# Attention rows in padded pairs, one division per tile, remainder loads doubled

## The chip, the cores and the metric

The kernel runs on one core of a Trainium2 chip. The metric is the device time of one execution in microseconds (us). Five engines work side by side, each in the order of its own instructions: TensorE (PE; its weight loads are listed as PEld), VectorE (DVE), ScalarE (ACT), GpSimd (POOL) and SyncE (SP), which here issues nearly all plain transfers. Engines wait for each other through semaphores.

## The reference

Pooled attention feeds a mixture of experts. All numbers are fp32.

```python
k_p = k.reshape(B, H, Sp, pool, D).mean(axis=3)        # 8, 8, 72, 64: eight rows pooled to one
v_p = v.reshape(B, H, Sp, pool, D).mean(axis=3)
scores = scale * np.matmul(q, k_p.transpose(0, 1, 3, 2))
attn = np.exp(scores - np.max(scores, axis=-1, keepdims=True))
attn = attn / (np.sum(attn, axis=-1, keepdims=True) + 1e-09)
x = np.matmul(attn, v_p)          # then (8, 8, 576, 64) -> x [4608, 512]
logits = x @ w_gate + modality_bias[modality_id]       # 8 experts
e_idx = np.argmax(logits, axis=1)                      # one expert per token
gate_w = softmax(logits)[e_idx]
out[mask_e] = gate_w * (np.maximum(x[mask_e] @ w1[e], 0.0) @ w2[e])   # 512 -> 1024 -> 512
```

q, k and v are 8 batches x 8 heads x 576 rows x 64.

## The kernel before, in words

The order of the work on each engine is the order in which the program is written; no scheduler moves it.

**Attention steps.** A tile is 128 rows of q for all eight heads. There are 36 tiles in 20 steps. A batch has 576 rows: 512 of them are four tiles in two steps (two tiles each), and the remaining 64 rows of two neighbouring batches make one mixed step with one tile. The main loop runs over the steps `n`. In iteration `n` it issues loads and stores (`loads(n)`), finishes step `n-1` (transposes of its probabilities `t_pe`, products with the pooled v `a_pe`, division `x_dve`) and carries step `n` and `n+1` through scores (`s_pe`), row maximum and subtraction (`s_dve`, L515 and L518) and exponentials (`s_act`).

**k and v.** Each batch's k and v come as a bulk load of 1024 KB (512 rows of all heads, L201 and L217) and a remainder load of the last 64 rows (`load_k4`, L208, 128 KB; `load_v4`, L224, twice 128 KB). GpSimd pools eight rows to one by three additions (`fold`, L296 to L298), VectorE pools a part (L301), and TensorE transposes the pooled k (`pk`, L330; L333 for the remainder) and v (`pv`, L362; L363). The two remainder tiles have one buffer each. Which loads stand in which iteration is given by the table `step_loads`; after them `loads(n)` issues the stores queued so far. SP issues all of these in order, and each transfer takes one of eight semaphores in turn, so a transfer is not issued before the one eight places ahead has landed.

**av and the division.** `a_pe` writes one tile's eight heads into two PSUM tiles of one bank each, `av0` and `av1` (four heads each; per head 64 values, 8 gate logits and the sum of the probabilities). `x_dve` divides each half by four VectorE instructions: L595 scales the sums, L597 takes their reciprocals `r`, L599 multiplies the values into the row buffer `xb`, L601 the logits into `lg`.

**Routing.** From `lg` small VectorE operations choose each token's expert, gate weight and place (L648 to L773). They wait in a list `drip`; `gap(n)` puts the next n of them into VectorE's order at that point. In `x_dve` a `gap(1)` stands before the reciprocal and another before the multiplication of each half.

**xs.** The rows of x go to a DRAM tile `xs` of 4608 rows, XW = 513 words each: 512 values and the gate weight, which four later transfers per group write in pieces of 4 bytes (L681, L683). A batch's 512 rows are stored at once, as 2048-byte pieces. The MoE gathers 128 rows at a time from `xs` by an indirect transfer.

**MoE.** Tokens are sorted into slots of 256 with one expert each. Per slot and per slice `f` of 128 hidden units TensorE does twelve hidden matmuls (`first`, L163: hp, in high and low parts), ScalarE writes `hh` (the high part of the rectified hidden values, L165), VectorE `hlo` (the rest, L167), and TensorE does six matmuls of the second layer (L1102: op). The hidden matmuls of slice f+1 stand ahead of the second-layer matmuls of slice f. The two hidden buffers are

```python
hp = [ps_av.tile([P, 512], F32, tag=f"av{i}", name=f"hp{i}") for i in range(2)]
```

The last slot (`end`) does its last five slices with the second layer of only half the tokens between them, and the other half behind.

Of the kernel before, what the change touches and what calls it, by code (L numbers as in the profile page):

```python
# [22 lines left out]
P = 128  # L23
# [7 lines left out]
def kernel(  # L31
# [25 lines left out]
    XW = D + 1  # L57
# [126 lines left out]
    with ExitStack() as actx:  # L184
# [21 lines left out]
        def load_k4(b):  # L206
            k4raw[b] = ap.tile([64, POOL * HD], F32, tag="k4", bufs=1, name=f"k4_{b}")
            nc.sync.dma_start(k4raw[b], rows_of(k, b)[NCH * P:, :])  # L208
# [261 lines left out]
        qts, pqs, scs, pes, pps, pts, avs, xb, lgs = {}, {}, {}, {}, {}, {}, {}, {}, {}  # L470
# [87 lines left out]
        def a_pe(t):  # L558
# [3 lines left out]
            av = [ps_av.tile([P, 512], F32, tag=f"av{u}", name=f"av_{t}_{u}") for u in range(2)]  # L562
# [5 lines left out]
            for u in range(2):  # L568
                for gg in range(2):
                    c = 2 * u + gg  # L570
                    for hs, y in halves:
                        nc.tensor.matmul(av[u][hs, 2 * VC * gg:2 * VC * (gg + 1)], pt[:, c, hs],  # L572
                                         vw[y][:, c].rearrange("p a x -> p (a x)"), start=(gg == 0), stop=False)
                dst4 = av[u][:, 0:4 * VC].rearrange("p (g x) -> p g x", g=2)[:, :, VC:2 * VC]
# [3 lines left out]
        def x_dve(t):  # L578
# [5 lines left out]
            if (gi in (0, 5)):  # L584
                xb[b] = late_p.tile([P, 4, D], F32, tag="xb", bufs=2, name=f"xb_{b}")
            if mixed:
                xb[b, 4] = late_p.tile([P, D], F32, tag="xb4", bufs=1, name=f"xb4_{b}")
            if gi == 0:
                lgs[g] = late_p.tile([P, GT, H, E], F32, tag="lg", bufs=2, name=f"lg_{g}")
            xo = xb[b, 4] if mixed else xb[b][:, gi % 5, :]  # L590
            for u in range(2):
                avv = av[u][:, 0:4 * VC].rearrange("p (h x) -> p h x", h=4)
                r = ap.tile([P, 4], F32, tag="r", bufs=4, name=f"r_{t}_{u}")
                rb = r.rearrange("p (h o) -> p h o", o=1)
                nc.vector.tensor_scalar(r, avv[:, :, VC - 1], float(POOL), 1e-9 * POOL, op0=ALU.mult, op1=ALU.add)  # L595
                gap(1)
                nc.vector.reciprocal(r, r)  # L597
                gap(1)
                nc.vector.tensor_tensor(xo[:, u * D // 2:(u + 1) * D // 2].rearrange("p (h d) -> p h d", h=4), avv[:, :, 0:HD],  # L599
                                        rb.to_broadcast([P, 4, HD]), op=ALU.mult)  # L600
                nc.vector.tensor_tensor(lgs[g][:, gi, 4 * u:4 * u + 4, :], avv[:, :, HD:HD + E],  # L601
                                        rb.to_broadcast([P, 4, E]), op=ALU.mult)

            if mixed:
                for z in range(2):
                    r0 = (b - 1 + z) * S + 512
                    stores.append(lambda z=z, r0=r0: nc.sync.dma_start(xs[r0:r0 + 64, 0:D], xo[64 * z:64 * z + 64, :]))
            if gi in (3, 8):
                stores.append(lambda: nc.sync.dma_start(
                    xs[b * S:b * S + 512, 0:D].rearrange("(p j) x -> p j x", j=4), xb[b]))  # L610
# [226 lines left out]
        for n, fn, b in ((0, load_k4, 1), (0, load_v4, 1), (0, load_k, 2), (0, load_v, 2), (0, load_k, 3), (1, load_q, 2),  # L837
                         (1, load_k4, 2), (1, load_v, 3), (1, load_k, 4), (2, load_qmix, 1), (2, load_v4, 2), (2, load_v, 4),
                         (3, load_k4, 3), (3, load_k, 5), (4, load_q, 3), (4, load_v4, 3), (4, load_v, 5), (5, load_k4, 4),
# [391 lines left out]
```

## Time and profile before

| | us |
|---|---|
| median of 3 runs | 654.39 (651.99 to 654.73) |
| profiled execution | 655.11 |
| its span | 653.4 |

| engine | busy us | share of the span |
|---|---|---|
| TensorE matmuls | 614.3 | 94% |
| TensorE weight loads | 557.2 | 85% |
| VectorE | 430.7 | 66% |
| ScalarE | 340.8 | 52% |
| GpSimd | 191.7 | 29% |

The span has two parts: attention with routing up to about 200 us, and the MoE slots behind it. Shares over the whole span mix the two, so each stage is read by itself. In rows of the timeline, the brackets say how long the engine had been idle and what ended that. TensorE's granted clock is 1.00 at full speed.

### The profile page before, as it was taken

To read this page: it belongs to the slowest core of one execution; us is meant where nothing else is said; L and a number is where in the kernel's file an instruction comes from. 1 tells how busy PE (TensorE), PEld (TensorE's weight loads), DVE (VectorE), ACT (ScalarE), POOL (GpSimd) and SP (SyncE) were. 2 spreads that over 40 slices of the span, in tenths; PEclk is the share of its full clock that TensorE was granted. 3 is DMA by queue.
4 is the path that set the end of the run, shared out by engine and by line. 5 is a ranking of instruction groups with operands and counts; after the bars stand their busy time and mean duration, and the time that the engine had idled before them with its cause. 6 is when DMAs were issued, how large, how long until landed. Compare 5 with 4: busy or idle time off the path is not lost.

```text
span 653.4 us, 12655 instructions
## 1 busy us (share of the span) xinstructions
PE 614.3 (94%) x4313; PEld 557.2 (85%) x4313; DVE 430.7 (66%) x963; ACT 340.8 (52%) x625; POOL 191.7 (29%) x228
## 2 busy tenths in 40 slices
PE   4499999899799999999999999999999999999993
PEld 3389898888698999999999999999999999999982
DVE  4577889899977665665565666566566656656540
ACT  2447665577451454454555555555555555555530
POOL 5388774753000211311211312220221221121121
PEclk9889999899999999999999999999999999999998
DMA  9999999995402821101101253101115410110120
GB/s 256 247 352 248 320 209 265 231 263 137 108 19 64 259 81 50 66 4 63 57 15 60 91 183 113 64 34 34 66 50 175 162 55 17 49 65 17 50 71 16
DMA packets 65404, 76.55 MB, mean 117 GB/s; under 512 B 15407, under 2 KB 42031, under 8 KB 65328
## 3 DMA queue, kind: packets, MB, share of 16 engines
q1 hardware_dynamic: 59088, 55.68, 32.0%
q0 software_dynamic: 6240, 19.95, 9.2%
q8 instruction: 36, 0.59, 0.4%
q14 instruction: 40, 0.33, 0.2%
HBM read 119.64 MB, written 19.42 MB: 213 GB/s over the span
## 4 chain that ended last, share of the span: by engine, by line
PE 70%; DMA 12%; DVE 7%; SPq 4%; issue 4%; POOL 1%; ACT 1%; POOLq 0%; DVEq 0%; ACTq 0%
PE op L1102 27%; PE hp L163 27%; DMA out_dram<-ob,sidx 7%; PE av L572 4%; DMA v<-in_v_dram 3%; PE xt L154 2%; PE sc L508 2%; PE ph L163 2%; PE av L576 2%; PE pp L537 1%; PE ptab L1008 1%; DVE hl L139 1%; DMA q<-in_q_dram 1%; PE pq L483 1%; SPq L241 1%
## 5 line engine op out<-in xcount | busy, mean ns | idle before, releaser
L136 ACT CAST hl<-raw 128x1024 fp32r<-128x1024 f32 x138 | 145.1, 1051 | 142.9 <-PE op L1102 140.9
L163 PE MATMUL hp<-xh,hl 128*128 128x256 f32 x1152 | 186.0, 284 | 0.4 <-issue 0.4
L163 PEld LDWEIGHTS hp<-xh,hl 128*128 128x128 f32 x1152 | 166.1, 189 | 11.5 <-issue 0.9
L139 DVE TENSOR_TENSOR hl<-raw,hl 128x1024 fp32r<-128x1024 f32 x144 | 174.9, 1216 | 0.0
L1102 PE MATMUL op<-hl,hh 128*128 128x512 f32 x556 | 174.2, 394 | 0.0
L1088 POOL DMA_INDIRECT out_dram<-ob,sidx x38 | 52.7, 1387 | 378.6 <-DVE ob L1084 269.7
L167 DVE SCALAR_TENSOR_TENSOR hlo<-hp,hh 128x256 fp32r<-128x256 f32 x139 | 58.9, 424 | 139.7 <-ACT hh L165 128.9
L1102 PE MATMUL op<-hl,hlo 128*128 128x512 f32 x278 | 108.9, 392 | 0.0
L1102 PEld LDWEIGHTS op<-hl,hh 128*128 128x128 f32 x556 | 95.2, 189 | 12.3
L163 PE MATMUL hp<-xl,hl 128*128 128x256 f32 x576 | 92.0, 282 | 0.0
L165 ACT ACTIVATE hh<-hp 128x256 fp32r<-128x256 f32 x139 | 53.2, 383 | 49.7 <-PE hp L163 47.8
L163 PEld LDWEIGHTS hp<-xl,hl 128*128 128x128 f32 x576 | 78.9, 190 | 0.0
L1102 PEld LDWEIGHTS op<-hl,hlo 128*128 128x128 f32 x278 | 52.2, 188 | 11.8
L572 PE MATMUL av<-vw,pt 128*128 128x146 f32 (+1 forms) x320 | 52.4, 307 | 3.0 <-DVE r L595 1.6
L143 POOL DMA_INDIRECT xg<-xs,gidx x40 | 42.8, 1071 | 17.8 <-issue 9.5
L572 PEld LDWEIGHTS av<-vw,pt 128*128 128x128 f32 (+1 forms) x320 | 41.5, 188 | 5.5 <-DVE lg L601 1.9
L508 PE MATMUL sc<-kt,qt 128*128 128x144 f32 x256 | 38.7, 296 | 1.4 <-DVE sb L518 1.3
L515 DVE TENSOR_REDUCE mx<-sc 128x8 f32<-128x576 f32 (+1 forms) x40 | 27.7, 693 | 15.4 <-ACT pt L556 8.6
L508 PEld LDWEIGHTS sc<-kt,qt 128*128 128x128 f32 x256 | 34.7, 198 | 2.2 <-issue 1.5
L157 DVE TENSOR_TENSOR xl<-xt,xh 128x512 fp32r<-128x512 f32 x38 | 24.6, 686 | 17.5 <-ACT xh L156 17.5
L542 ACT COPY pt<-pp 128x512 f32<-128x512 f32 x36 | 21.1, 585 | 28.6 <-PE pp L537 28.3
L576 PE MATMUL av<-vw,pt 128*128 128x146 f32 (+1 forms) x160 | 31.1, 299 | 0.5 <-ACT pt L556 0.5
(225 smaller groups left out, 716.9 us busy)
## 6 DMA issues: line engine op xcount, KB each, us to landing
raw<-in_moe_w_dram SPq DMA_DIRECT2D x304, 256.0 KB
xs<-xb SPq DMA_DIRECT2D x8, 1024.0 KB
k<-in_k_dram SPq DMA_DIRECT2D x7, 1024.0 KB
v<-in_v_dram SPq DMA_DIRECT2D x7, 1024.0 KB
q<-in_q_dram SPq DMA_DIRECT2D x6, 1024.0 KB
q<-in_q_dram SPq DMA_DIRECT2D x4, 512.0 KB
v<-in_v_dram SPq DMA_DIRECT2D x16, 128.0 KB
k<-in_k_dram SPq DMA_DIRECT2D x4, 256.0 KB
```

The lines of the kernel that those rows point to most:

```text
L136: nc.scalar.copy(hl[f][:, 0, :], raw[f])
L139: eng.tensor_sub(hl[f][:, 1, :], raw[f], hl[f][:, 0, :].bitcast(F32))
L143: nc.gpsimd.indirect_dma_start(out=xgs[(2 * s + tt) % len(xgs)], out_offset=None, in_=xs[0:rows, :], in_offset=IndirectOffsetOnAxis(idx[:, ...
L163: nc.tensor.matmul(ph, hl[f][:, w, d * P:(d + 1) * P], x[:, d, :], start=(n == 0 and d == 0), stop=(n == 2 and d == ND - 1))
L165: nc.scalar.activation(hh, ph, AF.Relu)
L167: nc.vector.scalar_tensor_tensor(hlo, ph, 0.0, hh.bitcast(F32), op0=ALU.max, op1=ALU.subtract)
L508: nc.tensor.matmul(dst, qt[:, i, :], kt[b % NB][:, :, h * SPL:(h + 1) * SPL], start=True, stop=True)
L515: nc.vector.reduce_max(mx, scv, axis=AX.X)
L572: nc.tensor.matmul(av[u][hs, 2 * VC * gg:2 * VC * (gg + 1)], pt[:, c, hs], vw[y][:, c].rearrange("p a x -> p (a x)"), start=(gg == 0), sto ...
L576: nc.tensor.matmul(dst4[hs], pt4[:, hs], v4[y][:, 2 * u:2 * u + 2, :], start=False, stop=True)
L1088: nc.gpsimd.indirect_dma_start(out=out[:, :], out_offset=IndirectOffsetOnAxis(idx.bitcast(U32), 0), in_=ob, in_offset=None, bounds_check=N ...
L1102: nc.tensor.matmul(o[tt], l[:, ts_], hl[f][:, w, D:2 * D], start=(f == 0 and n == 0), stop=(f == NF - 1 and n == 2))
```

## The change

It has five parts.

1. Rows of `xs` become 528 words wide. The row buffer `xb` becomes a tile [128, 2, 528] per step, eleven tiles in all; GpSimd sets their last 16 words to zero at the start, and each step stores its two tiles' rows as one transfer of 4224 contiguous bytes per partition. The store now writes the gate's word too, so gate transfers wait for it.
2. The remainder tiles of k and v get two buffers each. Their loads stand one batch earlier in the table, and those of batch 1 directly behind k and v of batch 1.
3. The routing inputs (`load_routing`, five small transfers of modality ids and bias) are loaded in iteration 1 and not before the loop, and their preparation on VectorE (`routing_constants_2`) moves from iteration 1 to 3.
4. `av` becomes one PSUM tile of two banks, and a tile's eight heads are divided by four instructions in place of eight. The routing operations stand behind them (`gap(4)`), not between.
5. The MoE's two hidden buffers become halves of one tile.

```diff
-    XW = D + 1
+    XW = D + 16
...
-            k4raw[b] = ap.tile([64, POOL * HD], F32, tag="k4", bufs=1, name=f"k4_{b}")
+            k4raw[b] = ap.tile([64, POOL * HD], F32, tag="k4", bufs=2, name=f"k4_{b}")
...
-            t4 = ap.tile([P, POOL * HD], F32, tag="v4", bufs=1, name=f"v4_{b}")
+            t4 = ap.tile([P, POOL * HD], F32, tag="v4", bufs=2, name=f"v4_{b}")
...
+        NX0 = 8
+        xbs = [cp.tile([P, 2, XW], F32, tag=f"raw{i}", name=f"xb{i}") for i in range(NX0)]
+        xbs += [late_p.tile([P, 2, XW], F32, name=f"xb{NX0 + i}") for i in range(3)]
+        for t in xbs:
+            nc.gpsimd.memset(t[:, :, D:XW], 0.0)
...
-            av = [ps_av.tile([P, 512], F32, tag=f"av{u}", name=f"av_{t}_{u}") for u in range(2)]
+            av = ps_av.tile([P, 2, 512], F32, tag="av", name=f"av_{t}")
...
+            xw = xbs[n if n < NX0 else NX0 + n % (len(xbs) - NX0)]
+            xo = xw[:, z, 0:D]
+            avv = av[:, :, 0:4 * VC].rearrange("p u (h x) -> p u h x", h=4)
+            r = ap.tile([P, 2, 4], F32, tag="r", bufs=4, name=f"r_{t}")
...
+            nc.vector.tensor_scalar(r, avv[:, :, :, VC - 1], float(POOL), 1e-9 * POOL, op0=ALU.mult, op1=ALU.add)
+            nc.vector.reciprocal(r, r)
...
+            gap(4)
...
+            elif z == 1:
+                jj = steps[n][1]
                 stores.append(lambda: nc.sync.dma_start(
-                    xs[b * S:b * S + 512, 0:D].rearrange("(p j) x -> p j x", j=4), xb[b]))
+                    xs[b * S:b * S + 512, :].rearrange("(p j) x -> p j x", j=4)[:, 2 * jj:2 * jj + 2, :], xw))
...
         load_gate()
         load_k(1)
+        load_k4(1)
         load_qmix(0)
         routing_constants()
         load_v(1)
+        load_v4(1)
         load_q(1, (0,))
         load_q(1, (1,))
-        load_routing()
...
-        for n, fn, b in ((0, load_k4, 1), (0, load_v4, 1), (0, load_k, 2), (0, load_v, 2), (0, load_k, 3), (1, load_q, 2),
+        for n, fn, b in ((0, load_k, 2), (0, load_k4, 2), (0, load_v, 2), (0, load_v4, 2), (0, load_k, 3), (1, load_q, 2),
...
-            if n == 1:
+            if n == 3:
                 routing_constants_2()
...
-    hp = [ps_av.tile([P, 512], F32, tag=f"av{i}", name=f"hp{i}") for i in range(2)]
+    hp2 = ps_av.tile([P, 2, 512], F32, tag="av", name="hp")
+    hp = [hp2[:, i, :] for i in range(2)]
```

How this moves instructions is seen at three places. The first is SP's order behind the load of k for batch 1 (`k_1` and `v_1` are the remainder tiles of batch 1, `qm` the mixed step's rows of q, `mod` and `mb` the routing inputs; DMAHW0 to 7 are the eight transfer semaphores). Before:

```order
L201 DMA k_169<-in_k_dram 128x4x512 [waits DMAHW5_49]
L241 DMA qm_171<-in_q_dram 64x8x64 [waits DMAHW6_49]
L241 DMA qm_171<-in_q_dram 64x8x64 [waits DMAHW7_49]
L217 DMA v_186<-in_v_dram 128x4x512 [waits DMAHW0_49]
L234 DMA q_188<-in_q_dram 128x8x128 [waits DMAHW1_49]
L234 DMA q_188<-in_q_dram 128x8x128 [waits DMAHW2_49]
L398 DMA mod<-in_moe_modality_id_dram 128x4x8 [waits DMAHW3_49]
L400 DMA mod<-in_moe_modality_id_dram 64x4x2 [waits DMAHW4_49]
L398 DMA mod<-in_moe_modality_id_dram 128x4x8 [waits DMAHW5_49]
L400 DMA mod<-in_moe_modality_id_dram 64x4x2 [waits DMAHW6_49]
L403 DMA mb<-in_moe_modality_bias_dram 128x16 [waits DMAHW7_49]
L208 DMA k_1_262<-in_k_dram 64x512 [waits DMAHW0_49,DVE_49]
```

And now:

```order
L201 DMA k_191<-in_k_dram 128x4x512 [waits DMAHW5_49]
L208 DMA k_1_193<-in_k_dram 64x512 [waits DMAHW6_49]
L241 DMA qm_195<-in_q_dram 64x8x64 [waits DMAHW7_49]
L241 DMA qm_195<-in_q_dram 64x8x64 [waits DMAHW0_49]
L217 DMA v_210<-in_v_dram 128x4x512 [waits DMAHW1_49]
L224 DMA v_1_212<-in_v_dram 64x1x512 [waits DMAHW2_49]
L224 DMA v_1_212<-in_v_dram 64x1x512 [waits DMAHW3_49]
L234 DMA q_215<-in_q_dram 128x8x128 [waits DMAHW4_49]
L234 DMA q_215<-in_q_dram 128x8x128 [waits DMAHW5_49]
L201 DMA k_282<-in_k_dram 128x4x512 [waits DMAHW6_49]
```

The remainder of k for batch 1 moves from behind the five routing transfers to directly behind k, that of v directly behind v.

The second is VectorE's order around one division with routing operations. Before, one tile (rows L650 to L658 are routing):

```order
L595 TENSOR_SCALAR r_0_1013<-av_0_986 128x4 [waits PE_49]
L650 TENSOR_REDUCE m_0_945<-lgr_943 128x9 [waits DVE_49]
L597 RECIPROCAL r_0_1013<-r_0_1013 128x4 [waits DVE_49]
L653 TENSOR_TENSOR lgr_943<-lgr_943,m_0_945 128x72 [waits DVE_49]
L599 TENSOR_TENSOR xb_1011<-av_0_986,r_0_1013 128x256 [waits DMAHW1_49,DVE_49]
L601 TENSOR_TENSOR lg_1012<-av_0_986,r_0_1013 128x32
L595 TENSOR_SCALAR r_1_1021<-av_1_987 128x4 [waits PE_49]
L657 SCALAR_TENSOR_TENSOR lgr_943<-lgr_943,w_166 128x72 [waits Activation_49]
L597 RECIPROCAL r_1_1021<-r_1_1021 128x4 [waits DVE_49]
L658 TENSOR_REDUCE m_0_946<-lgr_943 128x9 [waits DVE_49]
L599 TENSOR_TENSOR xb_1011<-av_1_987,r_1_1021 128x256 [waits DVE_49]
L601 TENSOR_TENSOR lg_1012<-av_1_987,r_1_1021 128x32
```

And now, one tile with the routing operations that follow it:

```order
L598 TENSOR_SCALAR r_1198<-av_1168 128x8 [waits PE_49]
L599 RECIPROCAL r_1198<-r_1198 128x8 [waits DVE_49]
L600 TENSOR_TENSOR xb_174<-av_1168,r_1198 128x512 [waits DVE_49]
L602 TENSOR_TENSOR lg_982<-av_1168,r_1198 128x64
L698 CAST rki_923<-rk_922 128x9
L699 TENSOR_SCALAR rkm_924<-rki_923 128x9 [waits DVE_49]
L700 TENSOR_SCALAR rki_923<-rki_923 128x9 [waits DVE_49]
L701 CAST rkf_925<-rkm_924 128x9
L702 CAST rh<-rki_923 128x9 [waits DVE_49]
```

Eight instructions with routing between them have become four with routing behind them.

The third is TensorE's order in the MoE, at two neighbouring slices. Before:

```order
L163 MATMUL hp_2867<-xh_2857,hl_2105 128x256 x4
L163 MATMUL hp_2867<-xl_2858,hl_2105 128x256 x4
L163 MATMUL hp_2867<-xh_2857,hl_2105 128x256 x4
L1102 MATMUL op_0_2864<-hl_1983,hh_2868 128x512 [waits Activation_49]
L1102 MATMUL op_0_2864<-hl_1983,hh_2868 128x512
L1102 MATMUL op_0_2864<-hl_1983,hlo_2870 128x512 [waits DVE_49]
L1102 MATMUL op_1_2865<-hl_1983,hh_2868 128x512 x2
L1102 MATMUL op_1_2865<-hl_1983,hlo_2870 128x512
L163 MATMUL hp_2866<-xh_2857,hl_2107 128x256 x4
```

And now:

```order
L163 MATMUL hp<-xh_87,hl_1750 128x256 [waits DVE_49]
L163 MATMUL hp<-xh_87,hl_1750 128x256 x3
L163 MATMUL hp<-xl_88,hl_1750 128x256 x4
L163 MATMUL hp<-xh_87,hl_1750 128x256 x4
L1107 MATMUL op_0_2664<-hl_1646,hh_2669 128x512 [waits Activation_49]
L1107 MATMUL op_0_2664<-hl_1646,hh_2669 128x512
L1107 MATMUL op_0_2664<-hl_1646,hlo_2671 128x512
L1107 MATMUL op_1_2665<-hl_1646,hh_2669 128x512 x2
L1107 MATMUL op_1_2665<-hl_1646,hlo_2671 128x512
L163 MATMUL hp<-xh_87,hl_1864 128x256 [waits DVE_49]
```

The wait for VectorE (for `hlo` of the slice before) has moved from the second-layer matmul that uses `hlo` up to the first hidden matmul of the next slice, since both hidden buffers are one tile.

More of the change, by code (lines that the diff above doesn't have):

```diff
@@ L583, in x_dve @@
             b = steps[n][0]
[L584 to L587, printed above, removed]
             if gi == 0:
                 lgs[g] = late_p.tile([P, GT, H, E], F32, tag="lg", bufs=2, name=f"lg_{g}")
[L590 to L602, printed above, removed]
@@ L609, in x_dve @@
+            gap(4)
+            if mixed:
+                for y in range(2):
+                    r0 = (b - 1 + y) * S + 512
+                    stores.append(lambda y=y, r0=r0: nc.sync.dma_start(xs[r0:r0 + 64, :], xw[64 * y:64 * y + 64, 0, :]))
+            elif z == 1:
+                jj = steps[n][1]
                 stores.append(lambda: nc.sync.dma_start(
-                    xs[b * S:b * S + 512, 0:D].rearrange("(p j) x -> p j x", j=4), xb[b]))
+                    xs[b * S:b * S + 512, :].rearrange("(p j) x -> p j x", j=4)[:, 2 * jj:2 * jj + 2, :], xw))
```

27 lines of the change are left out of this document (14 added, 13 removed).

## The prediction

> **What bounds the kernel now.** First the busy time by stages, in stretches that follow the stages (all views are of the kernel before; columns: stretch and length, then busy us of each engine with instructions, TensorE's granted clock, DMA share, GB/s):
>
> ```profile
> 20.00:40.00 20.00, 11.84 (x73) 9.84 (x71) 9.62 (x25) 6.68 (x18) 11.08 (x14) 0.74 0.95 293
> 40.00:85.00 45.00, 43.79 (x367) 40.52 (x366) 38.74 (x141) 29.52 (x79) 34.63 (x45) 1.00 1.08 300
> 85.00:121.00 36.00, 33.45 (x281) 29.74 (x279) 32.49 (x117) 23.34 (x61) 22.63 (x30) 1.00 1.12 236
> 121.00:140.00 19.00, 17.38 (x141) 15.97 (x141) 16.30 (x50) 12.08 (x31) 12.93 (x17) 0.91 0.97 195
> 140.00:180.00 40.00, 34.90 (x287) 31.61 (x289) 37.94 (x132) 24.81 (x61) 8.42 (x11) 0.96 0.57 158
> 180.00:640.00 460.00, 459.56 (x3115) 418.96 (x3112) 284.13 (x487) 236.50 (x361) 89.27 (x72) 1.00 0.23 72
> ```
>
> From 180 to 640 TensorE is never idle (0.44 us of 460), so nothing there can be gained by this change and every new wait costs in full. In 40 to 180 TensorE idles 1.21 + 2.55 + 1.62 + 5.10 = 10.5 us: that is the ceiling for faster divisions and stores, and in the last of these stretches VectorE is the fuller engine (37.94 of 40). In 20 to 40 TensorE idles 8.16 us and runs at clock 0.74. Second, who TensorE waited for (us in total, times, longest):
>
> ```profile
> PE pk L333 <- POOL kp L298: 6.2, 1, 6.2
> ...
> PE av L572 <- DVE r L595: 1.6, 1, 1.6
> PE av L572 <- DVE lg L601: 1.4, 3, 0.9
> PE pv L363 <- POOL vp L298: 1.1, 1, 1.1
> ```
>
> One wait of 6.2 us stands out. Third, the timeline around it (start, length, engine, line, tiles; SPq rows are the issuing queue), and the data rate from 15 to 50 us in 40 slices of 0.875 us:
>
> ```profile
> 19.86 3.76 SPq L398 DMA_DIRECT2D mod<-in_moe_modality_id_dram  x1
> 26.79 0.49 SPq L208 DMA_DIRECT2D k<-in_k_dram  x1
> 19.98 0.72 POOL L296 TENSOR_TENSOR k<-k 128x256 f32<-128x256 f32 x1 [1.53 <-DMA k<-in_k_dram]
> 29.85 0.72 POOL L296 TENSOR_TENSOR k<-k 64x256 f32<-64x256 f32 x1 [8.21 <-DMA k<-in_k_dram]
> 25.07 0.27 PE L330 MATMUL pk<-ident,kp 128*64 128x128 f32 x1 [0.21 <-DVE vw L383]
> 37.22 0.32 POOL L298 TENSOR_TENSOR vp<-v 128x64 f32<-128x64 f32 x1
> 31.53 0.31 PE L333 MATMUL pk<-ident,kp 64*64 64x64 f32 x1 [6.19 <-POOL kp L298]
> 31.78 1.34 PE L572 MATMUL av<-vw,pt 128*128 128x146 f32 x4
> 34.85 1.06 PE L537 MATMUL pp<-ident,pe 128*128 128x128 f32 x4
> 38.17 0.66 PE L572 MATMUL av<-vw,pt 128*128 128x146 f32 x4
> 39.66 0.60 PE L537 MATMUL pp<-ident,pe 128*128 128x128 f32 x4
> 41.43 0.38 PE L362 MATMUL pv<-ident,vp 128*128 128x128 f32 x2
> GB/s 288 384 349 177 220 246 328 380 341 297 291 284 126 20 23 188 197 159 363 391 332 372 398 393 400 386 377 362 364 356 314 222 272 360 386 389 384 362 212 182
> ```
>
> The remainder rows of k for batch 1 (the 64-partition load of L208) are issued at 26.79, behind five routing loads that hold SP from 19.86, and behind their dip in the rate (20 and 23 GB/s). GpSimd, idle for 8.21, folds them at 29.85, and TensorE's transpose starts at 31.53.
>
> **The early remainder load: -6.2, -1.6 and -1.1.** Now this load is the row behind k's own. GpSimd was waiting at 19.98 for exactly k's load, so k has landed by then; the remainder of 128 KB at some 300 GB/s (the slices above) comes 0.5 us later, GpSimd ends its present fold at 21.6 (1.34 us for the same three operations at 19.98 to 21.64) and has folded the remainder at about 23.3. TensorE asks for it at 25.34 (25.07 + 0.27). The 6.2 us go. After the stall the same work ran slow: from the four av matmuls at 31.78 to the four pp at 34.85 is 3.07 us, from 38.17 to 39.66 it is 1.49, so 1.58 us more go with the low clock. What is late next is v of batch 1. GpSimd's six fold operations for it follow those of k's remainder, from 31.5 to 37.54 (37.22 + 0.32), and TensorE transposes the result at 41.43, which would become 33.65. They can start once v has landed: behind k come now its remainder, the mixed rows of q and v itself, 0.13 + 0.26 + 1.05 MB, at some 0.3 MB per us 4.8 us after 19.98, so 24.8; folded by 30.9, 2.8 us to spare. q of batch 1 is pushed back by 0.39 MB, 1.3 us: the rate falls at 25.5, when all that was queued had landed, so q lands at about 26.8; its transposes stand just before the av matmuls at 38.17, that is at about 30: hidden. The 1.1 us at L363 is a later remainder of v, now loaded a batch earlier, and goes too: its fold was held by its load.
>
> The routing loads go to iteration 1, between the remainder of k for batch 3 and all of k for batch 4. Their dip, some 2.6 us (three slices), then delays loads needed three batches on: 0. Bounds: 0 to +2.6 us (one dip reaching TensorE once). SP now also waits for GpSimd and VectorE at the double-buffered tiles, whose earlier users (batch 0) are done by 18: 0.
>
> **The division: -1, between -5 and +4.** By form (count, busy us, mean ns, idle before):
>
> ```profile
> L518 DVE TENSOR_TENSOR sb<-sc,mx 128x576 f32<-128x576 f32 x30 | 22.6, 754 | 0.7
> L518 DVE TENSOR_TENSOR sb<-sc,mx 128x288 f32<-128x288 f32 x8 | 3.6, 453 | 0.1
> 89.42 0.15 DVE L595 TENSOR_SCALAR r<-av 128x4 f32<-128x4 f32 x1
> 89.49 0.17 DVE L695 CAST rki<-rk 128x9 int32<-128x9 f32 x1
> 89.61 0.18 DVE L597 RECIPROCAL r<-r 128x4 f32<-128x4 f32 x1
> ...
> 90.26 0.15 DVE L595 TENSOR_SCALAR r<-av 128x4 f32<-128x4 f32 x1
> ```
>
> A half takes 0.84 us from start to start (89.42 to 90.26), with or without a routing operation in it, because those start in the gaps that the dependent operations leave (89.49, before the reciprocal at 89.61). A tile is 1.68. From 288 to 576 elements L518 grows by 0.301 us, so 256 to 512 costs 0.27 more: the new tile takes 0.84 + 0.27 and some 0.05 for the wider small ones, 1.16, a saving of 0.52. With 36 tiles that is 18.7 us of VectorE, but most lies where TensorE is the bound. In routing stretches up to four operations of about 0.1 us lose their free places, so only 0.1 of the 0.52 is left: over some 20 tiles -2. Against that, TensorE's next av matmul was released by the first half, 0.84 after the start, and now by the whole tile, 1.16 after it: 0.3 later, wherever it waited closely (the lg rows of the wait list: 3, and about as many more with hardly any slack): +1. The lower end is half of the 10.5 us idle; the upper is twelve such tiles at 0.3.
>
> **Stores, padding, memsets: 0, between -3 and +4.** Wider rows make 3% more bytes. One contiguous store per step replaces 2048-byte pieces; the gate's four-byte writes stay, but the later ones now wait for the store just before, and SP stands in that wait ahead of k's and q's loads. These are one to two batches ahead, so 0; four such waits with 1 us each reaching TensorE are the upper end. Eleven memsets on GpSimd lie before its first fold, in its wait for v: 0.
>
> **The shared hidden tile: +4.8.** In the MoE the two hidden buffers become halves of one tile, and the first hidden matmul of every slice now carries a wait for VectorE (for hlo of the slice before):
>
> ```profile
> L167 DVE SCALAR_TENSOR_TENSOR hlo<-hp,hh 128x256 fp32r<-128x256 f32 x139 | 58.9, 424 | 139.7 <-ACT hh L165 128.9
> 312.87 0.43 DVE L167 SCALAR_TENSOR_TENSOR hlo<-hp,hh 128x256 fp32r<-128x256 f32 x1 [1.23 <-ACT hh L165]
> 313.40 0.41 PEld L163 LDWEIGHTS hp<-xh,hl 128*128 128x128 f32 x2
> 313.62 0.28 PE L163 MATMUL hp<-xh,hl 128*128 128x256 f32 x1
> 629.97 0.66 PEld L163 LDWEIGHTS hp<-xh,hl 128*128 128x128 f32 x4
> 631.26 0.42 DVE L167 SCALAR_TENSOR_TENSOR hx<-hp,hx 128x256 fp32r<-128x256 f32 x1 [3.81 <-ACT hx L165]
> 632.10 0.67 PEld L163 LDWEIGHTS hp<-xh,hl 128*128 128x128 f32 x4
> 632.25 0.43 DVE L167 SCALAR_TENSOR_TENSOR hx<-hp,hx 128x256 fp32r<-128x256 f32 x1 [0.57 <-ACT hx L165]
> ```
>
> In the steady loop hlo ends at 313.30, 0.10 before the weight load and 0.32 before the matmul: just hidden, 0. In the last slot the second matmuls cover only half as much: hx ends at 631.68 where the weight load now starts at 629.97 (+1.7 and, with the load no longer ahead of the matmul, +0.1), and at 632.68 against 632.10; the next three slices have the same gap of 0.58, of which some 0.5 shows each: 1.8 + 1.5 = 3.3. Slot 1, with routing still on VectorE, adds about 1, and three slices with hlo late by 0.3 the rest, estimates by the same gap: 4.8.
>
> **Sum**, against the profiled execution of 655.11 (span 653.4; median of the runs 654.39, 0.7 lower, which I leave): 655.1 - 6.2 - 1.6 - 1.1 - 1.0 + 4.8 = 650.0.
>
> **Rivals.** *The wait breaks the steady loop.* The load leads its matmul by 0.22 us (313.40, 313.62). If a matmul with a wait can't have its weights loaded ahead, 139 slices pay up to 0.22: +30.6, so 680; half of it gives 665. Decided by hlo's signal arriving later than 0.10 after its end. For: the margin is that thin. Against: in the kernel before the second-layer matmul on hlo carries such a wait, long satisfied, and its weights load ahead. *Another load takes the place of the stall.* v of batch 1, or a load behind SP's wait for a store, is late by most of what was won; the data rate near its ceiling until 140 speaks for it, the 2.8 us to spare against it: 650.0 + 6, 656. *More is won in the routing stretches.* A routing operation stalls inside a division:
>
> ```profile
> 97.33 2.32 DVE L722 TENSOR_SCALAR rot<-iota_f,e 128x8 f32<-128x8 f32 x1
> 97.26 2.35 POOL L296 TENSOR_TENSOR v<-v 128x1024 f32<-128x1024 f32 x1
> L686 DVE TENSOR_TENSOR cum<-cum,dc 128x8 bf16<-128x8 bf16 x3 | 2.4, 783 | 0.0
> ```
>
> If moving it behind the division, off the path of the av tile, saved the stall (2.3 and some 2 in cum), the time would be 645.5. But the operation ends at 99.65 and GpSimd's at 99.61: the stall goes with the neighbour, and then it holds the next row maximum. The Trainium skill ("SBUF — State Buffer", section "SBUF: two separate sides") states that VectorE and GpSimd share one port pair as an exclusive lock, held for the whole instruction; by that rule the move gains nothing here and the sum stays at 650.0, and the two ends 0.04 us apart agree.
>
> **How the numbers follow.** 0.5% is 3.3 us, about what a measurement can tell from no change: under 651.1 is faster, over 657.7 slower. The sum as it stands 0.50, own range 646 to 654 (0.32 faster, 0.18 same); the broken loop 0.13 (slower); another load 0.16 (half same, half slower); more won 0.17 (faster); the rest 0.04, split. So faster 0.51, same 0.26, slower 0.23. The range runs from 641 (more won, with the division's lower end) to 662 (another load, with the stores' upper end), leaving out most of the broken loop.
>
> **What would show it.** The wait of the L333 transpose on GpSimd gone and the clock of 20 to 40 near 1; the first transposes of v for batch 1 without a wait; a division of 1.1 to 1.2 us per tile; waits of hidden matmuls on VectorE in the last slot of about 3 us, and none in the middle. I am wrong if 300 to 600 us holds fewer slices than before, or if TensorE waits for a load before 140.

## The result: slower by 0.9%

| | before | changed |
|---|---|---|
| median of 16 runs, us | 654.69 | 660.75 |
| lowest and highest, us | 651.99, 665.57 | 657.44, 666.22 |
| profiled execution's span, us | 653.4 | 660.9 |
| ratio to before, with its 95% interval | | 1.0094 [1.0073, 1.0116] |

The forecast was 650.0, faster. The change is slower by about 6 us. Below, times of one session are compared by their ratio to runs of the kernel before in the same session, since its level moved between sessions (medians 654.7 to 658.7).

### The profile page after: what moved, and what is told of

It reads as the page before. It is cut to its first block, busy times and chain, and to the rows that moved or that the text cites. A ratio compares the mean times of both kernels' runs of the same rounds, so it can differ in the third digit from the quotient of the medians.

```text
span 660.9 us, 12527 instructions
## 1 busy us (share of the span) xinstructions
PE 620.1 (94%) x4313; PEld 561.1 (85%) x4313; DVE 428.6 (65%) x819; ACT 340.7 (52%) x625; POOL 193.1 (29%) x239
## 4 chain that ended last, share of the span: by engine, by line
PE 68%; DMA 13%; DVE 11%; issue 4%; ACT 2%; SPq 1%; POOL 1%; POOLq 0%; DVEq 0%; ACTq 0%
PE hp L163 27%; PE op L1107 26%; DMA out_dram<-ob,sidx 7%; DMA k<-in_k_dram 5%; PE av L579 3%; PE xt L154 2%; PE sc L515 2%; PE ph L163 2%; PE av L583 2%; DVE mx L522 1%; DVE sb L525 1%; DVE arow L704 1%; PE ptab L1013 1%; PE pp L544 1%; DVE hl L139 1%
## 5 line engine op out<-in xcount | busy, mean ns | idle before, releaser
L1107 PEld LDWEIGHTS op<-hl,hlo 128*128 128x128 f32 x278 | 52.2, 188 | 11.8
L579 PE MATMUL av<-vw,pt 128*128 128x146 f32 (+1 forms) x320 | 54.0, 312 | 2.1 <-DVE lg L602 1.8
L579 PEld LDWEIGHTS av<-vw,pt 128*128 128x128 f32 (+1 forms) x320 | 43.7, 195 | 4.3 <-DVE lg L602 2.3
L522 DVE TENSOR_REDUCE mx<-sc 128x8 f32<-128x576 f32 (+1 forms) x40 | 27.7, 693 | 18.1 <-ACT pt L563 11.3
L583 PE MATMUL av<-vw,pt 128*128 128x146 f32 (+1 forms) x160 | 32.1, 305 | 1.0 <-ACT pt L563 0.9
```

Of the source, the lines that this page charges most:

```text
L522: nc.vector.reduce_max(mx, scv, axis=AX.X)
L579: nc.tensor.matmul(av[hs, u, 2 * VC * gg:2 * VC * (gg + 1)], pt[:, c, hs], vw[y][:, c].rearrange("p a x -> p (a x)"), start=(gg == 0), sto ...
L583: nc.tensor.matmul(dst4[hs], pt4[:, hs], v4[y][:, 2 * u:2 * u + 2, :], start=False, stop=True)
L1107: nc.tensor.matmul(o[tt], l[:, ts_], hl[f][:, w, D:2 * D], start=(f == 0 and n == 0), stop=(f == NF - 1 and n == 2))
```

## The profile after

The same views as before the change. Stages first (stretch and length, busy us of each engine, granted clock, DMA share, GB/s):

```profile
20.00:40.00 20.00, 17.80 (x130) 15.50 (x129) 13.45 (x31) 11.55 (x32) 13.04 (x17) 0.91 1.07 295
40.00:85.00 45.00, 40.34 (x284) 36.84 (x283) 33.62 (x80) 23.02 (x61) 36.95 (x46) 0.85 1.02 323
85.00:121.00 36.00, 33.52 (x273) 30.59 (x271) 28.98 (x73) 21.42 (x54) 18.02 (x25) 0.95 0.78 246
121.00:140.00 19.00, 16.34 (x134) 14.87 (x135) 15.92 (x45) 9.97 (x26) 7.68 (x9) 0.91 0.37 110
```

From 20 to 40 us TensorE is now busy for 17.80 (11.84 before). But from 40 to 85, where it had been nearly full (43.79 at clock 1.00), it is busy for 40.34 at clock 0.85: fewer matmuls (284 for 367), at a lower speed. Who TensorE waited for:

```profile
PE sc L378 <- DVE sb L525: 6.4, 3, 2.6
PE pk L330 <- POOL kt L272: 4.7, 1, 4.7
PE pk L330 <- DVE kp L301: 3.9, 5, 1.4
PE sc L515 <- DVE sb L525: 2.2, 1, 2.2
...
PE hp L163 <- DVE hx L167: 1.6, 4, 0.9
...
PE hp L163 <- DVE hlo L167: 1.0, 1, 1.0
...
PE pq L490 <- DMA q<-in_q_dram: 0.8, 1, 0.8
```

The 6.2 us wait on the remainder of k is gone. In its place stand 8.6 us (6.4 + 2.2) on VectorE's subtraction of the row maximum (sb), where the same two waits were 1.6 us (0.3 + 1.3) in the kernel before, and 2.6 us in the MoE.

The gain and its loss can be followed iteration by iteration. Each iteration has one transpose of the remainder columns (`t4_pe`, the first matmul of line 549 in the kernel before, 556 now); its start, in us:

| iteration | 1 | 2 | 3 | 4 | 5 | 6 | 7 | 10 | 11 | 12 | 13 | 20 |
|---|---|---|---|---|---|---|---|---|---|---|---|---|
| before | 22.4 | 40.8 | 49.4 | 55.6 | 63.8 | 71.2 | 79.9 | 104.1 | 111.5 | 119.6 | 130.3 | 193.7 |
| changed | 22.4 | 34.1 | 42.2 | 48.4 | 62.9 | 70.3 | 83.1 | 108.3 | 116.7 | 129.0 | 136.5 | 197.0 |
| difference | 0.0 | -6.8 | -7.2 | -7.2 | -0.9 | -0.9 | +3.2 | +4.2 | +5.2 | +9.3 | +6.2 | +3.3 |

Iteration 2 begins 6.8 us earlier, and by iteration 4 the gain is 7.2, about what was forecast for the remainder loads. Then three iterations lose 6.3 (iteration 4), 4.1 (6) and 4.1 (11); the last batches get 6 us back, and attention ends 3.3 us late. The MoE adds 4.2: the end of TensorE's work is 7.5 us late.

**Iteration 4** has the preparation of the routing inputs: part 3 put it at the end of iteration 3, and VectorE reaches it at 47.96, as TensorE begins iteration 4. VectorE's timeline (start, length, what; in brackets the idle time before and what ended it), then TensorE's:

```profile
47.28 0.76 DVE L525 TENSOR_TENSOR sb<-sc,mx 128x576 f32<-128x576 f32 x1
...
48.82 0.18 DVE L427 TENSOR_SCALAR idw<-idt 128x36 bf16<-128x36 int32 x1
50.21 0.57 DVE L430 CAST mf<-mod 128x36 f32<-128x36 int32 x1 [1.21 <-DMA mod<-in_moe_modality_id_dram]
50.81 1.08 DVE L432 TENSOR_SCALAR mq<-mf 128x36 f32<-128x36 f32 x2
...
53.05 0.86 DVE L438 TENSOR_TENSOR bias_all<-bias_all,sc 128x288 f32<-128x288 f32 x1
...
54.17 0.74 DVE L522 TENSOR_REDUCE mx<-sc 128x8 f32<-128x576 f32 x1
54.95 0.76 DVE L525 TENSOR_TENSOR sb<-sc,mx 128x576 f32<-128x576 f32 x1
```

```profile
55.76 1.03 PE L378 MATMUL sc<-wgb,vt 128*128 128x32 f32 x4 [2.62 <-DVE sb L525]
...
57.29 1.34 PE L579 MATMUL av<-vw,pt 128*128 128x146 f32 x4
```

Between the subtraction at 47.28 and the next row maximum at 54.17 VectorE does nothing for the attention. It waits 1.21 us for a routing load, and its operations are slow (1.08 for the two comparisons of L432, 0.36 in the kernel before). TensorE waits 2.62 us, and then does its av matmuls at half speed (1.34 for four, 0.66 at full clock) until iteration 4's end; its granted clock from 55.76 to 62.91 is 0.52.

**Iterations 6 and 11** have the first routing operations of a group, in front of a subtraction. VectorE and GpSimd in iteration 6, and TensorE behind:

```profile
71.30 0.76 DVE L522 TENSOR_REDUCE mx<-sc 128x8 f32<-128x576 f32 x1 [1.43 <-ACT pt L563]
71.97 1.21 DVE L651 TENSOR_REDUCE lgr<-lg 128x72 f32<-128x576 f32 x1
73.22 2.40 DVE L652 TENSOR_TENSOR lgr<-lgr,bias_all 128x72 f32<-128x72 f32 x1
75.54 0.74 DVE L525 TENSOR_TENSOR sb<-sc,mx 128x576 f32<-128x576 f32 x1
```

```profile
73.18 2.34 POOL L296 TENSOR_TENSOR v<-v 128x1024 f32<-128x1024 f32 x1
```

```profile
76.34 1.06 PE L378 MATMUL sc<-wgb,vt 128*128 128x32 f32 x4 [1.86 <-DVE sb L525]
```

An addition of 72 elements lasts 2.40 us, as long as GpSimd's fold that began 0.04 us before it. The same happens at 119.66 (2.41, beside a fold at 119.64). In the kernel before this addition took 0.52 in iteration 6, behind a shorter fold that had begun earlier:

```profile
74.11 0.52 DVE L649 TENSOR_TENSOR lgr<-lgr,bias_all 128x72 f32<-128x72 f32 x1
```

**In the MoE**, the last slot (TensorE):

```profile
636.08 0.74 PE L163 MATMUL hp<-xh,hl 128*128 128x256 f32 x4 [0.88 <-DVE hx L167]
...
638.71 0.73 PE L163 MATMUL hp<-xh,hl 128*128 128x256 f32 x4 [0.23 <-DVE hx L167]
...
641.34 0.74 PE L163 MATMUL hp<-xh,hl 128*128 128x256 f32 x4 [0.24 <-DVE hx L167]
```

Each slice waits for VectorE. From slice to slice it is 2.63 us (638.71 to 641.34), for 2.13 in the kernel before (629.97 to 632.10 in the prediction's rows).

## The experiments

Four theories came from the two traces. H: the shared hidden tile costs the MoE 4 us. L: the late routing load cost iteration 4. C: GpSimd's folds meet routing operations and hold VectorE. D: the division with the routing behind it gives the gain back. A fifth, P, came later and stands with its run.

### Parts undone

**Two hidden tiles.** The av tile's pool is closed after the attention, and the hidden buffers get a pool of two tiles.

```diff
-    ps_av = ctx.enter_context(tc.tile_pool(name="ps_av", bufs=1, space=PSUM))
...
+        ps_av = actx.enter_context(tc.tile_pool(name="ps_av", bufs=1, space=PSUM))
...
+    ps_hp = ctx.enter_context(tc.tile_pool(name="ps_hp", bufs=1, space=PSUM))
...
-    hp2 = ps_av.tile([P, 2, 512], F32, tag="av", name="hp")
-    hp = [hp2[:, i, :] for i in range(2)]
+    hp = [ps_hp.tile([P, 512], F32, name=f"hp{i}") for i in range(2)]
```

> The changed kernel with part 5 undone: the two hidden buffers are two tiles of one PSUM bank each. Theory H (the shared tile costs the MoE): the waits of the hidden matmuls on hlo go, and with them what the two traces differ by between the first hidden slice (VectorE's hlo 3.3 us later than before) and the end (7.5 us later): about 4.2 us, so some 656.5, most of it in the last slot. Rival (the MoE is longer for another reason, such as rows of 528 words in the gather): less than 1 us.

Measured: median 656.66, ratio 1.0006 [0.998, 1.0033]. In its trace the MoE takes as long as before: the first hidden slices are 1.3 to 1.6 us late against before, the last 1.6. H holds, at 4.2 - 0.3 = 3.9 us by the traces.

**Routing inputs before the loop.** Part 3 undone.

```diff
         load_q(1, (1,))
+        load_routing()
...
-(1, load_routing, None),
...
-            if n == 3:
+            if n == 1:
                 routing_constants_2()
```

> The changed kernel with part 3 undone: the five routing loads stand before the loop again (behind q of batch 1) and are prepared in iteration 1. Theory L (VectorE stood until 50.21 behind a routing load that landed late, and TensorE ran on at a low clock): the 6.3 us that iterations 3 to 4 lost go, and about as much of the total, some 654.5; the 6.2 us wait on the remainder of k stays away. Rival C (VectorE is held later anyway, by GpSimd's folds and by routing operations in front of the row maxima, and takes the gain back): 2 us or less of the total. Rival S (these loads before the loop make the next loads late as before): a wait of TensorE on GpSimd's fold comes back.

Measured: 658.18, ratio 1.0004 [0.9974, 1.0034], 0.9% under the changed kernel. Iteration 4 takes 8.2 us as before, not 14.5. No wait on the remainder of k comes back. The size fits L; but whether the load's lateness or the place of the VectorE operations was the cost, this run does not separate (see below).

**Both.** The two edits together.

> Parts 3 and 5 undone together. If H and L both hold and add up: some 4.2 + 6.3 less than the changed kernel, about 650.5. If C holds in place of L: about 655.

Measured: 653.97, ratio 0.9946 [0.9916, 0.9977]. The two effects add up: 1.5% from the changed kernel. By the medians of these three runs, which were timed together, undoing part 5 is worth 4.2 us (658.18 to 653.97) and undoing part 3 2.7 us (656.66 to 653.97).

### GpSimd's folds

**The fold in pieces.**

```diff
-            nc.gpsimd.tensor_add(t[..., 0:256], t[..., 0:256], t[..., 256:512])
+            if len(t.shape) == 3:
+                for c in range(t.shape[1]):
+                    nc.gpsimd.tensor_add(t[:, c, 0:256], t[:, c, 0:256], t[:, c, 256:512])
+            else:
+                nc.gpsimd.tensor_add(t[..., 0:256], t[..., 0:256], t[..., 256:512])
```

> The changed kernel with GpSimd's first addition of a fold (128x1024 in one instruction, 2.35 us) cut into one instruction per 512 input words (128x256, 0.72 us each); all else as changed. Theory C (the routing additions of 2.40 us at 73.2 and 119.7 last as long as the GpSimd instruction they meet, and TensorE waits for the row maximum behind them): such operations end within about 0.8 us, and some 3 us of the total go. Rival (the operation waits for the whole fold, or the stretch has another cause): they still last 2 us or more, and the total stays within 1 us or grows by GpSimd's extra instructions.

Measured: 660.45, ratio 1.0049 [1.0002, 1.0096], not told apart from the changed kernel. The expected short hold did not come. VectorE and GpSimd of this kernel:

```profile
71.42 2.84 DVE L656 TENSOR_TENSOR lgr<-lgr,bias_all 128x72 f32<-128x72 f32 x1
```

```profile
71.40 2.77 POOL L298 TENSOR_TENSOR v<-v 128x256 f32<-128x256 f32 x4
74.25 1.26 POOL L301 TENSOR_TENSOR v<-v 128x512 f32<-128x512 f32 x1
```

The addition waits through all four pieces, which follow each other without a pause, and ends with the fourth. So cutting the fold is no remedy, and this run does not decide C.

**The routing operations behind the subtraction.** On top of parts 3 and 5 undone:

```diff
             nc.vector.reduce_max(mx, scv, axis=AX.X)
-            gap()
...
             scs[n, w] = sb
+            gap()
```

> Parts 3 and 5 undone, and in addition the two routing operations that stand between the row maximum and its subtraction are put behind the subtraction. Theory P (a routing operation held by a fold hurts where TensorE waits for the subtraction, not where it stands later): the waits of TensorE's score matmuls on the subtraction (7.6 us in the run with parts 3 and 5 undone) fall under 3 and the total by 3 or more, about 650. Theory C (the hold costs the same wherever it stands, since all of VectorE queues behind it): within 1 us of that run.

Measured: 656.24, ratio 0.9976 [0.9948, 1.0003] against 0.9946 with the gap in front. No gain; the addition of the first group now lasted 3.08 us. TensorE's waits on the subtraction did fall, from 7.6 to 2.0 us, but its waits on the division rose from 1.8 to 8.5. Theory P falls: VectorE is one queue, and held behind the subtraction it is held ahead of the next division.

### Parts alone

Parts 1 and 2 on the kernel before (part 2 needs the space that part 1 frees):

```diff
-    XW = D + 1
+    XW = D + 16
...
-tag="k4", bufs=1
+tag="k4", bufs=2
...
         load_k(1)
+        load_k4(1)
...
         load_v(1)
+        load_v4(1)
...
-        for n, fn, b in ((0, load_k4, 1), (0, load_v4, 1), (0, load_k, 2),
+        for n, fn, b in ((0, load_k, 2), (0, load_k4, 2), (0, load_v, 2),
...
```

> The kernel before with parts 1 and 2 alone (pair tiles with rows of 528 words, remainder tiles doubled and loaded early); the routing loads stay before the loop, division, routing places and hidden tiles as before. Beside the run of parts 1, 2 and 4 together (ratio 0.9946 to before) it differs in part 4 alone. Theory D (the early loads keep their gain of about 8 us, and the division in four instructions with the routing behind it gives most of it back): 0.988, some 647. Theory C (what gives it back are GpSimd's folds, which now run without pauses and meet the routing operations wherever these stand): 0.993 to 0.997, as with part 4.

Measured: 653.80, ratio 0.9931 [0.9898, 0.9965]. With part 4 it was 0.9946, in another session; the intervals overlap widely. Theory D falls, the division changes little.

Part 4 alone (the diff of the division as shown with the change, hidden buffers two tiles):

> The kernel before with part 4 alone: one two-bank tile for a tile's eight heads, four division instructions, routing behind them; hidden buffers two tiles of their own. Theory D: slower by 3 to 5 us (0.5 to 0.8%). The prediction's own term: -1, between -5 and +4.

Measured: 657.68, ratio 1.0001 [0.9965, 1.0038]. Neither gain nor loss.

Part 1 alone (the pair tiles and stores as shown with the change):

> The kernel before with part 1 alone: pair tiles, rows of 528 words, one contiguous store per step. The prediction's term: 0, between -3 and +4; packets of the stores take less time than the 213 to 319 ns after a store of before, and the data rate between 60 and 66 us lies over 250 GB/s in place of 152.

Measured: 661.85, ratio 1.0077 [1.005, 1.0104]. This was forecast as nothing. The stores themselves are better, as the data rate from 60 to 66 us shows, in the kernel before and with part 1 alone:

```profile
DMA packets 676, 0.91 MB, mean 152 GB/s; under 512 B 16, under 2 KB 447, under 8 KB 676
```

```profile
DMA packets 1493, 2.00 MB, mean 334 GB/s; under 512 B 66, under 2 KB 1090, under 8 KB 1493
```

But that is what does the harm, as the runs with GpSimd held back show below. In the kernel before, GpSimd waited 3.61 us for a remainder of v that was stuck behind a store (the fold at 71.11), and so came to the next v fold at 80.14, after the routing operations of iteration 6, of which L657 took 0.22 us:

```profile
71.11 0.73 POOL L296 TENSOR_TENSOR v<-v 128x256 f32<-128x256 f32 x1 [3.61 <-DMA v<-in_v_dram]
...
80.14 2.36 POOL L296 TENSOR_TENSOR v<-v 128x1024 f32<-128x1024 f32 x1
```

With part 1 alone it does not wait, and meets them. The same operation (L660 here) is held through two GpSimd operations that follow each other (VectorE, GpSimd, TensorE of this kernel):

```profile
75.96 2.84 DVE L660 SCALAR_TENSOR_TENSOR lgr<-lgr,w 128x72 f32<-128x72 f32 x1
```

```profile
75.80 0.60 POOL L357 TENSOR_TENSOR vw<-vp,m 128x256 f32<-128x256 f32 x1
76.37 2.34 POOL L296 TENSOR_TENSOR v<-v 128x1024 f32<-128x1024 f32 x1
```

```profile
79.55 0.77 PE L577 MATMUL av<-vw,pt 128*128 128x146 f32 x4 [2.51 <-DVE lg L603]
```

Part 5 alone (one hidden tile on the kernel before, in a pool of its own):

```diff
+    ps_hp = ctx.enter_context(tc.tile_pool(name="ps_hp", bufs=1, space=PSUM))
...
-    hp = [ps_av.tile([P, 512], F32, tag=f"av{i}", name=f"hp{i}") for i in range(2)]
+    hp2 = ps_hp.tile([P, 2, 512], F32, name="hp")
+    hp = [hp2[:, i, :] for i in range(2)]
```

> The kernel before with part 5 alone: the hidden buffers are halves of one tile. Prediction's term: +4.8 us, with nearly nothing in the steady loop and some 3.3 in the last slot; by the run of the changed kernel with this part undone, +4.2. So 1.0055 to 1.008.

Measured: 662.21, ratio 1.0027 [0.9989, 1.0066]; its runs spread from 655 to 666, so the ratio doesn't decide. In its trace the first hidden slice is 2.2 us late against before (attention, which this edit does not touch, so spread between executions: iteration 6 took 13.5 us for 8.7) and the end 7.0: 4.8 us in the MoE. TensorE's waits there:

```profile
PE hp L162 <- DVE hx L166: 2.1, 4, 1.4
...
PE hp L162 <- DVE hlo L166: 1.0, 1, 1.0
```

### GpSimd held back

If C is right, making GpSimd wait must make the kernel faster. Two copies of one gate column, each of 128 numbers that are ready only after the routing operations, are put ahead of the folds of v for batches 4 and 6; GpSimd's order then waits there.

```diff
+        held_v = ap.tile([P, 1], F32, name="held_v")
...
+                    if b + 1 in (4, 6):
+                        at(hook_0, m, lambda b=b: nc.gpsimd.tensor_copy(held_v, gate[:, 9 * (b - 3) // 2:9 * (b - 3) // 2 + 1]))
                     at(hook_0, m, lambda b=b: pool_v(b + 1))
```

With part 1 alone:

> The kernel before with part 1 alone, and GpSimd held back at two places: ahead of the folds of v for batches 4 and 6 it copies one column of gate weights, so that these folds begin after the routing operations of their iteration. Nothing else. Theory C (part 1 alone cost 0.77% because stores no longer delay the loads, so that the fold of 2.35 us meets a routing operation in front of TensorE's wait): holding GpSimd back gives most of it back, ratio to before 0.997 to 1.001. Rival (part 1 costs by its stores, its wider rows or its waits): it stays at 1.006 to 1.009, or grows since v comes later.

Measured: 649.89, ratio 0.9871 [0.9811, 0.9931], from 1.0077 without the hold. GpSimd and VectorE of this kernel:

```profile
79.11 0.19 POOL L793 COPY held_v<-gate 128x1 f32<-128x1 f32 x1 [3.36 <-DVE gate L681]
79.25 2.36 POOL L296 TENSOR_TENSOR v<-v 128x1024 f32<-128x1024 f32 x1
```

```profile
74.13 0.23 DVE L652 TENSOR_TENSOR lgr<-lgr,bias_all 128x72 f32<-128x72 f32 x1
...
76.26 0.22 DVE L660 SCALAR_TENSOR_TENSOR lgr<-lgr,w 128x72 f32<-128x72 f32 x1
```

GpSimd waits 3.36 us, and the operation that lasted 2.84 lasts 0.22. C holds: a wait added to GpSimd takes about 2% off the time. That is more than was expected, which was only to get back what part 1 had cost. The trace shows where: iterations 6 and 11 take 8.1 and 7.7 us (11.8 and 11.3 without the hold), and iteration 12 takes 7.3 where the kernel before took 10.7, since that kernel has a meeting of its own there (an addition of eight numbers at 119.46 lasts 1.98 us beside a fold; here it lasts 0.14).

With the whole change:

> The whole change with the same hold of GpSimd. Theory C: the routing additions of 2.40 us at 73 and 119.7 are short again and the total falls by 4 to 6 us from the changed kernel, ratio to before about 1.001 to 1.004; what stays is the shared hidden tile (4 us) and the routing load (some 5). Rival: unchanged at 1.007 to 1.012.

Measured: 653.01, ratio 0.9905 [0.9874, 0.9935], from 1.0094; again more than expected. The two iterations that lost 4.1 us each now take 8.4 and 8.4 (before: 8.7 and 8.1).

With parts 1 and 2:

> Parts 1 and 2 alone with the same hold of GpSimd. Theory C: the two routing operations of 2.4 us are short again, the total falls by 4 to 6 us from the run of parts 1 and 2 (0.9931) to 0.984 to 0.987. Rival: within 0.3% of 0.9931.

Measured: 644.97, ratio 0.9804 [0.9745, 0.9863]. This beats both kernels. The expected 0.984 to 0.987 lies partly inside the interval.

The same, but with the preparation of the routing inputs in iteration 3 as in the change, their loads staying before the loop:

> As the run before, with the preparation of the routing inputs on VectorE in iteration 3 in place of 1 (their loads stay before the loop). In the run of parts 1 and 2 these operations met GpSimd's folds at 34 to 39 (3 us longer) and iteration 2 lost 2.4 us. If that is the cause, 2 us less than the run before, 0.981 to 0.984; if they meet other folds in iteration 3, no difference.

Measured: 649.12, ratio 0.9855 [0.9796, 0.9913], 4.15 us over the run before it in the same session: the opposite of what was expected. VectorE, GpSimd and TensorE:

```profile
48.95 1.83 DVE L432 TENSOR_SCALAR mq<-mf 128x36 f32<-128x36 f32 x2
...
53.65 0.74 DVE L520 TENSOR_REDUCE mx<-sc 128x8 f32<-128x576 f32 x1
```

```profile
48.84 1.82 POOL L296 TENSOR_TENSOR k<-k 128x768 f32<-128x768 f32 x1
```

```profile
55.24 1.06 PE L378 MATMUL sc<-wgb,vt 128*128 128x32 f32 x4 [2.18 <-DVE sb L523]
```

No load is waited for, and yet the row maximum comes at 53.65 (54.17 in the changed kernel) and iteration 4 takes 14.4 us (14.5). So theory L in its first form falls: the load was 1.21 us late, but the cost is the place. Some ten VectorE operations in front of a row maximum on which TensorE waits, stretched by GpSimd's folds, are enough.

The kernel before with the hold alone:

> The kernel before with the hold of GpSimd alone. If the late remainder load of v already did what the hold does (its wait of 3.61 us at 71.11 put the fold of v behind the routing operations), the ratio is 0.997 to 1.003, and the gain of part 1 with the hold (0.9871) belongs to its stores. If the hold alone is the gain, 0.986 to 0.992.

Measured: 657.09, ratio 0.9986 [0.9959, 1.0013]: no gain from the hold alone. Its trace has two sides. In iteration 12 the hold parts the kernel's own meeting, and it takes 7.1 us for 10.7. But iteration 6 takes 11.7 us for 8.7: GpSimd waited 4.89 us for the late remainder of v and TensorE 2.72 us behind it, before the held fold, and the hold itself waited only 0.41 us there. This wait differs between executions. In the four traces with the stores of before (the kernel before, part 4 alone, this run, part 5 alone) GpSimd waits 3.61, 4.14, 4.89 and 6.61 us, and TensorE 1.15, 1.96, 2.72 and 4.21. So in iteration 6 the late load does the work of the hold, but at a price of its own. The gain of part 1 with the hold needs its stores, which take that wait away.

Parts 1, 2 and 4 with the hold:

> Parts 1, 2 and 4 with the hold of GpSimd; it differs from the run of parts 1 and 2 with the hold (0.9804) in the division alone, now that no fold meets a routing operation there. The prediction's term for the division was -1 us, between -5 and +4; if its gain was hidden by the folds, the ratio is 0.973 to 0.978; if the later release of the av tile costs, 0.983 or more; if both cancel, within 0.3% of 0.9804.

Measured: 647.86, ratio 0.9816 [0.9749, 0.9882] against 0.9804. The division's worth stays too small for these runs. In this execution the preparation of the routing inputs met GpSimd's folds (its two comparisons took 1.90 us at 35.77, 0.27 in the run without part 4) and iteration 2 took 12.9 us; in the run without part 4 they did not meet, and it took 8.1. So such meetings also differ from run to run, and the medians of these kernels spread by them.

## Why the prediction was wrong, by its own steps

The parts, from ratios along one chain of runs (each step carries about 0.3% to 0.5%): part 1 +0.77%, part 2 -1.46% (1.0077 to 0.9931), part 4 +0.15% (to 0.9946), part 3 +0.60% (to 1.0006), part 5 +0.88% (to 1.0094). The forecast was a gain of 5.1 us, and the change lost 6.2. Of these 11 us, 9 are the two terms put at nothing, the routing loads (0.60%) and the stores (0.77%).

- **"-6.2, -1.6 and -1.1": right, the last by a mechanism that was only half seen.** The wait on the remainder of k and the one at the remainder of v are gone; 7.2 us were won by iteration 3, against 7.8 forecast for the first two, and part 2 measured -1.46%, about 9.6 us. The 1.1 was read from one execution, the mildest of the four traces (1.15 to 4.21 us), and the stores of part 1 alone already take this wait away: in the trace of part 1 the transposes at L363 start without a wait.
- **"The routing loads ... 0": the step that failed first.** It costed the five loads, and of the preparation that moves with them not one instruction. These ten or so operations stood at the end of iteration 1 in the kernel before, on VectorE from 40.80 until the next row maximum at 44.12, and cost TensorE little there; at the end of iteration 3 they stand ahead of a row maximum for which TensorE waits. Priced by the runs: 0.60% along the chain, 4.15 us between the two runs with GpSimd held (whose iteration 4 took 14.4 and 8.7). The bound of 2.6 us was for a late load and bounded the wrong thing.
- **"Stores, padding, memsets: 0, between -3 and +4": failed too.** Part 1 alone measured +0.77%, 5 us, with an interval of 3.3 to 6.8 that only touches the upper end. That end stood for waits of SP, and they are not the cause: with GpSimd held the same stores cost nothing (0.9871). The working left out what a faster transfer triggers: it removed a wait of GpSimd that had kept a long fold apart from the routing operations.
- **"The division: -1": not contradicted.** 1.0001 alone, and its interval of some 2.4 us either way cannot tell -1 from 0. A tile takes 1.17 us from its first start to the next instruction's, 1.16 was worked out (VectorE, changed kernel):

```profile
55.62 0.16 DVE L598 TENSOR_SCALAR r<-av 128x8 f32<-128x8 f32 x1
55.82 0.20 DVE L599 RECIPROCAL r<-r 128x8 f32<-128x8 f32 x1
56.05 0.69 DVE L600 TENSOR_TENSOR xb<-av,r 128x512 f32<-128x512 f32 x1
56.66 0.21 DVE L602 TENSOR_TENSOR lg<-av,r 128x64 f32<-128x64 f32 x1
56.79 0.75 DVE L522 TENSOR_REDUCE mx<-sc 128x8 f32<-128x576 f32 x1
```

- **"The shared hidden tile: +4.8": right.** 4.2 us in the changed kernel, 3.9 by undoing it, 4.8 alone in the traces. In the changed kernel 2.7 of it fall in the last slot (3.3 forecast, of which the 0.5 per slice came out) and 1.5 before (1.5 forecast). In the steady loop nothing, as worked out from the 0.10 us between hlo's end and the weight load: from slice to slice the shift against before stays at 4.5 to 4.9 us from 228 to 620 us.
- **The rivals.** "More is won in the routing stretches" was rejected for the right reason: the stall goes with GpSimd's instruction. But the consequence was not drawn. If the neighbour sets the stall, then whatever moves the neighbour in time moves the stall, and the change moved GpSimd in two ways, by earlier loads and by faster stores. "Another load takes the place" put the loss where it was not: no wait of TensorE on a load exceeds 0.8 us in the changed kernel.
- **The range, 641 to 662,** holds the measured 660.75 by luck. Its upper end stood for a load late by 6 us together with SP's waits at the stores, neither of which occurred; and 656 + 4 is 660, not 662.

How much of each lost iteration is the wait, and how much the low clock behind it, can be estimated from the granted clock of the changed kernel. In iteration 4 the wait is 2.62 us, and 7.15 us at clock 0.52 cost 3.4 more: 6.0 of the 6.3. In iteration 6 it is 1.86 and 3.4 (6.78 us at 0.50), less the 1.15 that the kernel before lost there to the remainder of v: 4.1 of 4.1. In iteration 11 the waits are 1.87, 0.20 and 0.49, and 6.16 us at 0.72 cost 1.7: 4.3 for 4.1. Of the 6 us that the last batches regain, 3.1 are iteration 12 (10.7 to 7.5), where the addition that met a fold in the kernel before (1.98 us at 119.46) lasts 0.11.

What stays open: where the rest of these 6 us comes from, and how much the late routing load adds to the new place of its operations.

## What to carry to other kernels

Where two engines hold each other up, their phase is a resource: a load that comes early, a store that gets faster or an operation that is moved can bring two long instructions together, and one small wait put in on purpose can be worth more than all of it (here 1.3% to 2.0% in three kernels, and nothing in the kernel before). When an edit moves a load, count everything that moves with it on every engine, and read at its new place who waits behind it. Halves of one tile are one tile to the dependence tracking: look for where the cover is thin, here only the last slot.

## What the hardware showed that was not expected

A VectorE operation that meets a GpSimd addition waits longer than that one instruction if the next follows without a pause: 2.84 us through four independent pieces of 0.69 us each (2.77 for the four), and 2.84 us through the two of 0.60 and 2.34 us shown with part 1 alone. In both places it got in where GpSimd's next operation depends on the one before; that this is the reason is not shown. The Trainium skill ("SBUF — State Buffer", section "Who interferes with whom") states that a VectorE instruction with two operands in SBUF contends with a GpSimd instruction that reads SBUF, that the loser blocks for the whole instruction, and that reductions never contend here. By that rule the addition should have been free after one piece; the trace shows otherwise, and it decides. On reductions the trace agrees: L651 took 1.21 us at 71.97, 1.20 in the kernel before, with GpSimd busy beside it both times.

TensorE's matmuls ran at half speed for some 7 us after a wait of 2.62 us (from 55.76 until iteration 4's end at 62.91), so this wait cost some 6 us, well over twice its length. Behind the wait of 1.86 us in iteration 6 the granted clock was 0.50 for 6.78 us; behind that of 1.87 us in iteration 11 it was 0.72 over 6.16 us, so the price is not the same each time.
